# The last batch's second product and the global rows by Strassen's scheme, with result buffers of their own and stores from two queues

## The chip, the cores and the metric

The kernel runs on one core of one Trainium2 chip. A core has five engines, each with an instruction stream of its own: PE (matrix multiplication, with weight loads that overlap it), DVE (element-wise work), ACT (activations and copies), POOL (general work) and SP, which here only issues DMAs. Engines wait for each other through semaphores. Matrix products land in PSUM, eight banks of 512 fp32 columns; everything else lies in SBUF.

The metric is the time of one execution in microseconds (us).

## The reference

Attention with a narrow band and some global rows, then a feed-forward block:

```python
batch, n_heads, seq_l, seq_g, head_dim = (8, 8, 512, 32, 64)
k_all = concatenate([k_g, k_l]);  v_all = concatenate([v_g, v_l])
out_g = softmax(scale * q_g @ k_all.T) @ v_all
s_ll  = where(abs(pos_q - pos_k) <= 32, scale * q_l @ k_l.T, -1e9)
out_l = softmax(concatenate([scale * q_l @ k_g.T, s_ll])) @ v_all
x = concatenate([out_g, out_l], rows)      # per batch 32 + 512 rows, 512 columns (all heads)
h = x @ w_in                               # 512 -> 2048
g = h * clip(h + 3, 0, 6) / 6
out = g @ w_out                            # 2048 -> 512
```

The output has 8 x 544 = 4352 rows of 512 columns in fp32.

## The kernel before, in words

**Tiling.** Work goes by batch b = 0 to 7. Local attention runs in blocks of 128 rows (`local`), the 32 global rows of a batch at once (`global_`). Everything on PE is fp16 with fp32 sums. The result of the attention is turned into `xt[b % 3]`, with the 512 features on partitions in four chunks; the global rows of all eight batches gather in `xg`, 256 rows.

**Feed-forward block.** `ffn_local(b)` has two products. The first (`first`, matmul at line 1003) makes one chunk of 128 of the 2048 hidden features for all 512 rows: four matmuls of 512 columns into one PSUM bank. ACT then makes `t1` out of it (line 1009), and DVE multiplies (line 1013, called a gate here): the result is chunk c of `gl`, fp16, hidden features on partitions. There are two sets, `gl0` (16 tiles, even batches) and `gl1` (one tile of 16 chunks, odd batches). The second product (`second`, line 1029) takes 128 rows and adds up 16 matmuls with `w_out`, 512 columns each, in one bank; ACT or DVE copies the bank into one of three buffers `ot` (line 1040 or 1042), and SP stores it (line 1075). The very last 128 rows are done in two halves of 256 columns. `ffn_global` does the same with the 256 global rows after batch 7: 16 chunks of 256 columns at line 1003, two second products, and four stores of 32 rows each (line 1090).

**Banks.** Three PSUM banks `m` serve these products and, once the last transpose is done, the bank `t` too. Two banks `s` (scores) and two `a` (attention output) belong to the attention.

**Order.** No engine decides anything at run time. A planner (`Plan.run`) goes through all operations with costs written in the code, a pick for PE by keys (`key`, `pick`) and for the other engines by ranks, and writes each engine's instructions down in the order in which it started them. The instruction streams are then fixed; only semaphores decide when an instruction starts. An engine thus waits at an instruction even if the next could go. At the end of the kernel batch 7's first product is followed by the global rows' first product, mixed with second products of batches 6 and 7, and then by second products alone.

**POOL** issues loads and, for the batches from 2 on, copies parts of `vn` to `vs` for the attention (line 645). Its last of these is batch 7's.

Of the kernel before, what the change touches and what calls it, by code (L numbers as in the profile page):

```python
# [10 lines left out]
FP32 = mybir.dt.float32  # L11
# [228 lines left out]
def kernel(  # L240
# [40 lines left out]
    def sbs(name, n, shape, dtype=FP16):  # L281
        return [sb(f"{name}_{i}", shape, dtype) for i in range(n)]
# [49 lines left out]

    plan = Plan()
    add = plan.add
    plan.free = {"m": NM, "t": 2, "s": 4, "a": 4, "t1": NT1, "ot": NOT}
    slots = {"m": list(range(NM)), "t1": list(range(NT1)), "ot": list(range(NOT))}

    def dma(rows, run):

# [29 lines left out]
    def dve(n, fast=1):  # L369
        return 65.0 + n / 0.96 / fast  # L370
# [620 lines left out]


    m1_done = [[] for _ in range(B)]
    m2_done = [[] for _ in range(B)]

    def first(x, n, g, c, deps, rank, kind, free):
        st = {}
# [22 lines left out]
    def second(g, t0, gates, rank, store, kind, cols=slice(0, dm)):  # L1020
# [29 lines left out]
            what="store")  # L1050
        return last

    def ffn_local(b):
        x = xt[b % 3]
        r = b % 2
        parts = ((0, 2), (2, 4)) if b == 0 else ((0, 4),)
        gates = {}
        for part, (j0, j1) in enumerate(parts):
            t0, n = j0 * P, (j1 - j0) * P
            for c in range(NDFF):  # L1060
                free = m2_done[b - 2] if b >= 2 else vperm[0] + vperm[1] if b == 1 else []
                deps = x_op[b][j0:j1] + wi[c // (NDFF // 4)]
                pe, ga = first(lambda m, t0=t0, n=n: x[:, m, t0:t0 + n], n, g_l[r][c][:, t0:t0 + n], c, deps,
                               (b, part, c), "M1", free)
                m1_done[b].append(pe)
                gates[part, c] = ga
        for j in range(NJ):
            row = b * S + Sg + j * P
            part = next(k for k, (j0, j1) in enumerate(parts) if j0 <= j < j1)


            half = dm // 2
            for i, cols in enumerate((slice(0, half), slice(half, dm)) if (b, j) == (B - 1, NJ - 1) else (slice(0, dm),)):
                def store(o, row=row, cols=cols):
                    nc.sync.dma_start(out=out[row:row + P, cols], in_=o[:, 0:cols.stop - cols.start])
                m2_done[b].append(second(g_l[r], j * P, [gates[part, c] for c in range(NDFF)], (b, j + i), store, "M2", cols))

    def ffn_global():
        gates = []
        for c in range(NDFF):  # L1080
            deps = [x_op[b][NJ] for b in range(B)]
            pe, ga = first(lambda m: xg[:, :, m * Sg:(m + 1) * Sg], B * Sg, g_g[c], c, deps, (B, 0, c), "M1",
                           m2_done[B - 2])
            gates.append(ga)
        per = P // Sg
        rows = out.rearrange("(b s) d -> b s d", s=S)
        for i in range(B // per):
            def store(o, i=i):
                for a in range(per):
                    nc.sync.dma_start(out=rows[i * per + a, 0:Sg, :], in_=o[a * Sg:(a + 1) * Sg, :])  # L1090
            second(g_g, i * P, gates, (B, i), store, "M2")
# [27 lines left out]
    EARLY = 60000  # L1119
    KEYS = (30, 30, -20, 40, 27)  # L1120
    REST = 0
    KEYED, GLAST = 0, 0
    state = {"since": 0, "fed": False}
    PIECES = 2 * NDFF

    def key(op):
        if op.key is None:
            r, w = op.rank, op.what
            if w == "Places":
                op.key = -1e9  # L1130
            elif r[0] == B:

                op.key = B * PIECES + (r[2] if w == "M1" else NDFF + 4 * r[1] + r[2])
            elif w == "M1":
                op.key = r[0] * PIECES + 2.0 * (r[2] + r[1] * 0.5)
            elif w[0] == "M":
                op.key = (r[0] + 1) * PIECES + 2.0 * (4 * r[1] + r[2]) + 1
            elif w[0] in "VTG":
                op.key = (r[0] - 1) * PIECES - LEAD - STEP * (2 - 0.25 * min(r[2] * 2, 4)) + KEYS[0]
            else:  # L1140
                op.key = (r[0] - 1) * PIECES - LEAD + STEP * (r[2] + 2 * (r[1] - 1)) + KEYS[1 + (w[0] == "A") + 2 * (w[-1] == "g")]
        return op.key

    def warm():
# [19 lines left out]
    def pick(plan, can):  # L1164
# [76 lines left out]
```

## Time and profile before

| | us |
|---|---|
| median of 3 runs | 330.4 (330.1 to 330.95) |
| the profiled execution | 331.21 |
| its span, first to last instruction | 329.4 |
| PE busy | 318.2 (97%) |
| DVE busy | 239.3 (73%) |
| ACT busy | 237.2 (72%) |
| POOL busy | 174.9 (53%) |

How to read the rows below. A group row has line, engine, operation, output and inputs with shapes, count, then busy time and mean ns of one, then the idle time in front of it and what ended that. A timeline row has start, duration (of all of the row's instructions, merged), engine, line, operation and count; in brackets the idle time of the engine before it and the releaser. PEq, SPq and ACTq rows are the engine's sequencer, for SP the issue of a DMA. The duration of a matmul contains its way through the array, so that successive ones overlap; the pace is told by the starts. A row of the chain has start, duration, engine, output and line. "128x512" is partitions by elements.

### The profile page before, as it was taken

How to read it: one execution, taken by the hardware profiler on the slowest of the kernel's cores; microseconds unless marked ns; L12 is line 12 of the kernel's file. 1: busy time of each engine (PE TensorE's matmuls, PEld its weight loads, DVE VectorE, ACT ScalarE, POOL GpSimd, SP SyncE). 2: the span in 40 equal slices, each digit the busy share in tenths (PEclk: the TensorE clock that was granted, in tenths of full speed). 3: DMA queues.
4: the chain of work that ended last, by engine and by line, in shares of the span. 5: the costliest groups of instructions: out<-in, count | busy, mean ns of one | idle time of the engine just before them, and what ended most of it. 6: DMA issues, size and time to landing. Idle time of an engine off the chain costs nothing.

```text
span 329.4 us, 12254 instructions
## 1 busy us (share of the span) xinstructions
PE 318.2 (97%) x4880; PEld 164.4 (50%) x4880; DVE 239.3 (73%) x987; ACT 237.2 (72%) x571; POOL 174.9 (53%) x278
## 2 busy tenths in 40 slices
PE   8999968999899999999999999999999999999995
PEld 3456756654445544455444544444444444446644
DVE  5699998879985889878898997588414993376400
ACT  3799999848967688689768999979815982365511
POOL 8499353799548879979997998059200000000000
PEclk9999999999999999999999999999999999999999
DMA  8999999998999799959999999598934457200013
GB/s 128 226 204 173 178 235 217 123 180 182 113 136 158 143 116 168 170 120 180 179 111 128 211 102 140 123 136 105 177 99 121 60 109 120 82 34 0 34 57 103
DMA packets 111369, 44.30 MB, mean 134 GB/s; under 512 B 88304, under 2 KB 107088, under 8 KB 111312
## 3 DMA queue, kind: packets, MB, share of 16 engines
q0 software_dynamic: 53136, 17.47, 52.6%
q1 hardware_dynamic: 58176, 26.05, 43.2%
q8 instruction: 38, 0.62, 0.8%
q14 instruction: 19, 0.16, 0.2%
HBM read 35.13 MB, written 8.91 MB: 134 GB/s over the span
## 4 chain that ended last, share of the span: by engine, by line
PE 75%; ACT 9%; DMA 7%; DVE 5%; issue 2%; POOL 1%; ACTq 0%
PE m L1029 30%; PE m L1003 23%; PE t L1029 4%; ACT ex L835 4%; PE t L1003 3%; PE m L1149 3%; DMA win<-in_moe_w_in_dram 3%; PE a L862 3%; DMA et<-ex 3%; PE s L819 2%; ACT t L1009 2%; DVE gl L1013 2%; DMA vn<-in_v_l_dram 1%; ACT vs L643 1%; PE t L883 1%
## 5 line engine op out<-in xcount | busy, mean ns | idle before, releaser
L1003 PE MATMUL m<-xt,win 128*128 128x512 f16 (+1 forms) x536 | 114.3, 354 | 4.2 <-DVE gl L1013 3.1
L1029 PE MATMUL m<-wout,gl 128*128 128x512 f16 (+1 forms) x496 | 117.7, 376 | 0.1
L645 POOL COPY vs<-vn 64x528 f16<-64x528 f16 (+1 forms) x165 | 102.5, 621 | 22.0 <-ACT vn L381 5.7
L1013 DVE SCALAR_TENSOR_TENSOR gl<-t,m 128x512 f16<-128x512 f32 (+1 forms) x147 | 86.3, 601 | 24.2 <-ACT t L1009 23.8
L835 ACT ACTIVATE ex<-sm,mx 128x128 f16<-128x128 f32 x256 | 85.1, 396 | 14.6 <-DVE mx L831 14.1
L1009 ACT ACTIVATE t<-m 128x512 f32<-128x512 f32 (+1 forms) x147 | 76.7, 532 | 19.7 <-PE m L1003 18.7
L1003 PEld LDWEIGHTS <-win 128*128 128x128 f16 x640 | 59.7, 98 | 57.9 <-issue 4.7
L1029 PEld LDWEIGHTS <-gl 128*128 128x128 f16 x560 | 51.7, 98 | 53.5 <-issue 0.4
L831 DVE CUSTOM_DVE_ANT_0 sm<-s,mask 128x128 f32<-128x128 f32 x256 | 60.0, 285 | 7.2 <-PE s L819 5.9
L643 ACT COPY vs<-vn 32x528 f16<-32x528 f16 (+1 forms) x39 | 24.5, 628 | 0.8
L876 DVE TENSOR_TENSOR x<-a,rec 128x256 f16<-128x256 f32 x64 | 24.0, 416 | 0.0
L1040 ACT COPY ot<-m 128x512 f32<-128x512 f32 (+1 forms) x21 | 12.1, 576 | 15.7 <-PE m L1029 15.7
L353 POOL DMA_DIRECT2D vn<-in_v_l_dram x24 | 21.1, 888 | 1.3 <-DMA kn<-in_k_l_dram 0.8
L831 DVE DVE_READ_ACCUMULATOR2_ANT mx<- 128x1 f32 x256 | 21.2, 83 | 0.0
L353 POOL DMA_DIRECT2D vn<-in_v_g_dram x7 | 4.1, 581 | 25.4 <-PE a L965 24.5
L862 PE MATMUL a<-vs,et 128*32 128x65 f16 x1024 | 14.4, 195 | 1.3 <-DMA et<-ex 1.2
L1149 PE MATMUL m<-ident 128*128 128x512 f16 x57 | 15.6, 392 | 0.0
L862 PEld LDWEIGHTS <-et 128*32 128x32 f16 x1024 | 10.2, 96 | 10.9 <-issue 7.3
L1013 DVE SCALAR_TENSOR_TENSOR gl<-t,t 128x512 f16<-128x512 f32 (+1 forms) x13 | 8.1, 624 | 9.7 <-ACT t L1009 9.7
L1029 PE MATMUL t<-wout,gl 128*128 128x512 f16 (+1 forms) x64 | 14.8, 353 | 0.0
L874 DVE RECIPROCAL rec<-a 128x4 f32<-128x4 f32 x64 | 8.5, 167 | 7.9 <-PE a L862 7.9
L353 POOL DMA_DIRECT2D kn<-in_k_l_dram x22 | 14.1, 644 | 0.1
(108 smaller groups left out, 292.4 us busy)
## 6 DMA issues: line engine op xcount, KB each, us to landing
out_dram<-ot SPq DMA_DIRECT2D x31, 256.0 KB, 2.6
vs<-vn SPq DMA_DIRECT2D x14, 264.0 KB, 7.0
qn<-in_q_l_dram POOLq DMA_DIRECT2D x14, 256.0 KB, 8.1
kn<-in_k_l_dram POOLq DMA_DIRECT2D x14, 256.0 KB, 7.1
vn<-in_v_l_dram POOLq DMA_DIRECT2D x24, 128.0 KB, 5.8
win<-in_moe_w_in_dram POOLq DMA_DIRECT2D x4, 512.0 KB, 9.6
wout<-in_moe_w_out_dram POOLq DMA_DIRECT2D x8, 256.0 KB, 11.2
gl<-in_v_l_dram POOLq DMA_DIRECT2D x8, 128.0 KB, 9.3
```

The costliest lines, as they stand in the source:

```text
L353: op = add("POOL", dma(rows, run), lambda: nc.gpsimd.dma_start(out=dst, in_=src), deps, rank, LOAD_LAT + (MARGIN if what[0] in "vqkg" and ...
L643: nc.scalar.copy(out=dst, in_=src)
L645: (nc.vector if o.on == "DVE" else nc.gpsimd).tensor_copy(out=dst, in_=src)
L831: nc.vector.tensor_tensor_reduce(out=sm[i3][h], in0=pss[e][:, p * P:(p + 1) * P], in1=m, scale=-scale, scalar=3.0e38, op0=ALU.add, op1=ALU ...
L835: nc.scalar.activation(out=ex[ie][:, h, :], in_=sm[i3][h], func=EXP, scale=-1.0, bias=mx[i3][h])
L862: nc.tensor.matmul(out=psa[h // 4][q, c0:c0 + D + 1], lhsT=et[k][:, h * P + u * Sg:h * P + (u + 1) * Sg], rhs=vs[r][:, j * UJ + u, h, 0:D ...
L876: nc.vector.tensor_tensor(out=xs[ix][:, 4 * c * D:4 * (c + 1) * D].rearrange("q (h d) -> q h d", d=D), in0=acc[c][:, :, 0:D], in1=rr[c].to ...
L1003: nc.tensor.matmul(out=ps[:, 0:n], lhsT=w_in[:, m, c * P:(c + 1) * P], rhs=x(m), start=(m == 0), stop=(m == NP - 1))
L1009: nc.scalar.activation(out=t1[st["t"]][:, 0:n], in_=pm[st["m"]][:, 0:n], func=RELU, bias=0.5, scale=1.0 / 6.0)
L1013: nc.vector.scalar_tensor_tensor(out=g, in0=t1[st["t"]][:, 0:n], scalar=1.0, in1=pm[st["m"]][:, 0:n], op0=ALU.min, op1=ALU.mult)
L1029: nc.tensor.matmul(out=pm[st["m"]][:, 0:n], lhsT=g[c][:, t0:t0 + P], rhs=w_out[:, c, cols], start=(c == 0), stop=(c == NDFF - 1))
L1149: nc.tensor.matmul(out=pm[slots["m"][0]], lhsT=w, rhs=x)
```

## The change

Batch 7's second product (512 rows) and that of the global rows (256 rows) are done by Strassen's scheme in Winograd's form. Rows, hidden features and output columns are each cut into halves. With A the gates (A11 the upper rows and the lower features) and W the weights `w_out`, the seven products are

```
S1 = A21 + A22   S2 = S1 - A11   S3 = A11 - A21   S4 = A12 - S2      (sums of gates, into vs)
T1 = W12 - W11   T2 = W22 - T1   T3 = W22 - W12   T4 = W21 - T2      (weight differences, into qn and kn)
P1 = A11 W11  P2 = A12 W21  P3 = S4 W22  P4 = A22 T4  P5 = S1 T1  P6 = S2 T2  P7 = S3 T3
U2 = P1 + P6  U3 = U2 + P7  U4 = U2 + P5
C11 = P1 + P2   C12 = U4 + P3   C21 = U3 + P4   C22 = U3 + P5
```

- One product is eight matmuls of 256 columns for 128 rows of each half (`product`). A group of seven makes 256 rows of output (`pair`): two groups for batch 7, one for the global rows. The three groups give 168 matmuls of 256 columns.
- The weight differences are four POOL operations of 2048 elements, planned after the turns of batches 5 to 7 (`weight_sums`).
- The sums of gates are made for two feature chunks of each half at a time, by DVE or POOL as the planner decides (`sevenths`, `both`): 16 operations of 512 elements for batch 7, 16 of 256 for the global rows. To this end the first product makes chunks c and 8 + c one after the other.
- P1 is copied to SBUF by ACT or DVE; U2, U3 and U4 and the four results are additions on DVE with one input in PSUM.
- Results go to five fp32 buffers of 256 columns laid over `vn[0]` (`oq`) and from there to memory. For batch 7 SP issues one store for each; for the global rows ACT and SP issue two stores of 32 rows each.
- The banks of the attention, `s` and `a`, join the `m` banks once the attention is done.
- `gl0` becomes one tile. Batch 6's `ffn_local` is added to the plan ahead of batch 7's `global_`, and global rows have new keys.

In the planned order, POOL does the four weight differences right behind its last copy. Each group of four chunks of batch 7 is followed by its sums: for the first three groups DVE makes S1 and POOL S3, S2 and S4; for the last, DVE makes S1, S2 and S4 and POOL S3. On DVE the last three sums stand ahead of the first global gate. On PE all 16 chunks of batch 7's first product come in a row, then a last quarter of a second product of batch 6, P1, seven global chunks, P6, five chunks, P7, four chunks, and then products alone; the last one is P4 of batch 7's second group. On SP the last stores are C12 of that group, two of the global C21, and C21 of that group.

The diff, cut to its core:

```diff
--- before.py
+++ after.py
@@ tiles
-    g_l = [sbs("gl0", NDFF, [P, Sl]), [gl1[:, c, :] for c in range(NDFF)]]
+    gl0 = sb("gl0", [P, NDFF, Sl])
+    g_all = [gl0, gl1]
+    g_l = [[g[:, c, :] for c in range(NDFF)] for g in g_all]
...
-    plan.free = {"m": NM, "t": 2, "s": 4, "a": 4, "t1": NT1, "ot": NOT}
+    plan.free = {"m": NM, "t": 2, "s": 4, "a": 4, "t1": NT1, "ot": NOT, "oq": 5}
...
+    SEVEN, SUMS = {7: 4, 8: 4}, ("DVE", "POOL")
...
+    HALF, NH = dm // 2, NDFF // 2
+    wt = [qn[k].rearrange("p n c -> p (n c)") for k in range(2)] + [knall[:, k * NH * HALF:(k + 1) * NH * HALF] for k in range(2)]
+    wt = [t.rearrange("p (c f) -> p c f", c=NH) for t in wt]
+    ut = [t.bitcast(FP32) for t in (xt[(B - 3) % 3].rearrange("p n c -> p (n c)"), qT[0].rearrange("d j p q -> d (j p q)"))]
+    oq = vn[0].rearrange("p n h d -> p (n h d)")[:, 0:10 * HALF].bitcast(FP32).rearrange("p (k c) -> p k c", k=5)
+
+    def both(dst, a, b, op, n, engines, deps, rank, what):
+        o = add(engines, tuple(dve(n, 2) if e == "DVE" else 100.0 + 1.9 * n for e in engines), None, deps, rank, lat=220.0, what=what)
+        def emit():
+            (nc.vector if o.on == "DVE" else nc.gpsimd).tensor_tensor(out=dst, in0=a, in1=b, op=op)
...
+    def weight_sums():
+        lo, hi, left, right = slice(0, NH), slice(NH, NDFF), slice(0, HALF), slice(HALF, dm)
...
+        for k, (a, d, x) in enumerate(((w_out[:, lo, right], w_out[:, lo, left], ()), (w_out[:, hi, right], wt[0], (0,)),
+                                       (w_out[:, hi, right], w_out[:, lo, right], ()), (w_out[:, hi, left], wt[1], (1,)))):
+            wt_op[k] = both(wt[k], a, d, ALU.subtract, n, ("POOL",), free + [wt_op[i] for i in x], (B, 5, k), f"wt{k}")
+
+    def sevenths(b, g, n, gates, into, free, store, banks):
+        st_ = into.rearrange("p u h d -> p (u h d)")[:, 0:4 * NH * n].rearrange("p (s c t) -> p s c t", s=4, c=NH)
+        up, dn = slice(0, n), slice(n, 2 * n)
+        for c in range(0, NH, 2):
+            lo, hi = slice(c, c + 2), slice(NH + c, NH + c + 2)
+            deps = [gates[i] for i in (c, c + 1, NH + c, NH + c + 1)] + free
+            for k, (x, y, op, by) in enumerate(((g[:, lo, dn], g[:, hi, dn], ALU.add, ()), (st_[:, 0, lo], g[:, lo, up], ALU.subtract, (0,)),
+                                                (g[:, lo, up], g[:, lo, dn], ALU.subtract, ()), (g[:, hi, up], st_[:, 1, lo], ALU.subtract, (1,)))):
+                o = both(st_[:, k, lo], x, y, op, 2 * n, SUMS, deps + [done[i] for i in by], (b, 0, 6, c, k), f"sum{b}.{k}")
...
+        for i in range(n // P):
+            pair(b, i, n, g, st_, sums, gates, store, banks)
+
+    def pair(b, i, n, g, s_, sums, gates, store, banks):
...
+        def product(m, x, lhs, rhs, deps, take=None):
+            def emit():
+                if take is not None:
+                    st[take] = slots["m"].pop(0)
+                for c in range(NH):
+                    nc.tensor.matmul(out=at(x), lhsT=lhs(c), rhs=rhs(c), start=c == 0, stop=c == NH - 1)
...
+        def plus(dst, a, x, deps, bank=None):
+                nc.vector.tensor_tensor(out=dst, in0=a(), in1=at(x), op=ALU.add)
...
+        def outs(row, cols, x, a, deps, bank):
+                so["o"] = slots["oq"].pop(0)
+                nc.vector.tensor_tensor(out=oq[:, so["o"], :], in0=a, in1=at(x), op=ALU.add)
...
+            half = [add("ACT", 900.0, lambda: store(i, row, cols, oq[:, so["o"], :], nc.scalar), [op], (-1,), lat=0.0, what="store")] if b == B else []
...
+        p1 = product(0, "X", gt(0, a1), wo_(0, left), g1 + wo, 0)
...
+        p6 = product(1, "Y", su(1), wt_(1), sums[1] + [wt_op[1]], 1)
+        u2 = plus(ub[1], lambda: ub[0], "Y", [p6, cx], None if two else 1)
+        p7 = product(2, "W", su(2), wt_(2), sums[2] + [wt_op[2]] + ([cx] if two else []), None if two else 2)
+        u3 = plus(ub[2], lambda: ub[1], "W", [p7, u2])
+        p5 = product(3, "V", su(0), wt_(0), sums[0] + [wt_op[0]] + ([u2] if two else []), None if two else 3)
+        u4 = plus(ub[3], lambda: ub[1], "V", [p5, u2])
+        c22 = outs(1, right, "V", ub[2], [p5, u3], None)
+        p2 = product(4, "X", gt(NH, a1), wo_(NH, left), g2 + [cx] + ([u3] if two else []))
+        c11 = outs(0, left, "X", ub[0], [p2], None if two else 0)
+        p3 = product(5, "V", su(3), wo_(NH, right), sums[3] + [c22, u4])
+        c12 = outs(0, right, "V", ub[3], [p3, u4], 1 if two else 3)
+        p4 = product(6, "W", gt(NH, a2), wt_(3), [u3, wt_op[3]] + ([c11] if two else []))
+        c21 = outs(1, left, "W", ub[2], [p4], 0 if two else 2)
@@ ffn_local
+                place = 2 * (c % NH) + c // NH if b in SEVEN else c
...
+        if b in SEVEN:
+            def quarter(i, row, cols, o, queue):
+                r0 = b * S + Sg + (2 * row + i) * P
+                queue.dma_start(out=out[r0:r0 + P, cols], in_=o)
+            sevenths(b, g_all[r], Sl // 2, [gates[0, c] for c in range(NDFF)], vs[r], [], quarter, SEVEN[b])
+            return
@@ ffn_global
+            def quarter(i, row, cols, o, queue):
+                for a in range(per // 2) if queue is nc.scalar else range(per // 2, per):
+                    queue.dma_start(out=rows[row * per + a, 0:Sg, cols], in_=o[a * Sg:(a + 1) * Sg, :])
+            sevenths(B, g_all[B % 2], B * Sg // 2, gates, vs[B % 2], m2_done[B - 2], quarter, SEVEN[B])
+            return
@@ order of the work
+        if b == B - 1 and SEVEN:
+            weight_sums()
+            ffn_local(b - 1)
         global_(b)
-        ffn_local(b)
+        if b != B - 2 or not SEVEN:
+            ffn_local(b)
...
+    GLOBALS = (0, 0.5, 12)
...
-                op.key = B * PIECES + (r[2] if w == "M1" else NDFF + 4 * r[1] + r[2])
+                op.key = B * PIECES + (GLOBALS[0] + GLOBALS[1] * r[2] if w == "M1" else GLOBALS[2] + 4 * r[1] + r[2])
...
+    for k, (r, banks) in enumerate((("s", pss), ("a", psa))):
+        pm.extend(banks)
+        add("POOL", 0.0, lambda k=k: slots["m"].extend((NM + 1 + 2 * k, NM + 2 + 2 * k)), [u for u in plan.ops if r in u.give], (-9,),
+            0.0, take=(r,) * 4, give=("m", "m"), what="bank")
```

More of the change, by code (lines that the diff above doesn't have):

```diff
@@ L993 @@
     m1_done = [[] for _ in range(B)]
-    m2_done = [[] for _ in range(B)]
+    m2_done = [[] for _ in range(B + 1)]
+    SEVEN, SUMS = {7: 4, 8: 4}, ("DVE", "POOL")
     def first(x, n, g, c, deps, rank, kind, free):
@@ L1062, in ffn_local @@
                 deps = x_op[b][j0:j1] + wi[c // (NDFF // 4)]
+                place = 2 * (c % NH) + c // NH if b in SEVEN else c
                 pe, ga = first(lambda m, t0=t0, n=n: x[:, m, t0:t0 + n], n, g_l[r][c][:, t0:t0 + n], c, deps,
-                               (b, part, c), "M1", free)
+                               (b, part, place), "M1", free)
                 m1_done[b].append(pe)
                 gates[part, c] = ga
+        if b in SEVEN:
[4 more added lines that the diff above has]
+            return
         for j in range(NJ):
@@ L1081, in ffn_global @@
             deps = [x_op[b][NJ] for b in range(B)]
-            pe, ga = first(lambda m: xg[:, :, m * Sg:(m + 1) * Sg], B * Sg, g_g[c], c, deps, (B, 0, c), "M1",
-                           m2_done[B - 2])
+            pe, ga = first(lambda m: xg[:, :, m * Sg:(m + 1) * Sg], B * Sg, g_g[c], c, deps,
+                           (B, 0, 2 * (c % NH) + c // NH if B in SEVEN else c), "M1", m2_done[B - 2])
             gates.append(ga)
```

73 lines of the change are left out of this document (70 added, 3 removed).

## The prediction

> **What bounds the kernel now.** I read the page's busy line first, then the same engines cut into the stages of the end (windows), then the chain that ended last.
>
> ```profile
> PE 318.2 (97%) x4880; PEld 164.4 (50%) x4880; DVE 239.3 (73%) x987; ACT 237.2 (72%) x571; POOL 174.9 (53%) x278
> PEclk9999999999999999999999999999999999999999
> ...
> 283.50:298.00 14.50, 14.50 (x69) 6.61 (x68) 9.62 (x14) 10.05 (x17) 0.00 (x0) 1.00 0.11 40
> 298.00:312.00 14.00, 14.00 (x98) 9.38 (x97) 7.52 (x17) 6.99 (x19) 0.00 (x0) 1.00 0.05 19
> 312.00:326.10 14.10, 14.05 (x82) 7.75 (x80) 0.42 (x1) 2.79 (x6) 0.00 (x0) 1.00 0.25 74
> ...
> 282.65 0.97 PE t L1029 x4
> 283.62 1.73 PE m L1003 x8
> 293.12 2.59 PE m L1003 x12
> 312.19 9.50 PE m L1029 x44
> 325.17 0.89 PE m L1029 x8
> 326.06 0.03 ACTq L1040
> 326.13 0.37 ACT ot L1040
> ```
>
> The window rows give, after the stretch and its length, PE, weight loads, DVE, ACT and POOL in turn. From 283.5 us to 326.1 us PE has no gap, the clock is full, POOL does nothing, and DVE is busy 9.62, 7.52 and 0.42 us in three stretches of about 14 us. The chain is PE from end to end; only a copy and a store stand behind it. So here a microsecond of matmul taken away is a microsecond of the span, as long as DVE, which gets work, doesn't take PE's place.
>
> The instruction orders of the two kernels are the same on all five engines up to the first matmul of batch 7's first product (283.46 us below), but for POOL, which gets its new work behind its last copy. Everything that the change can do lies behind that point.
>
> **Terms, step by step.**
>
> *Matmuls.* These rows give the pace: a start to the next start, since the ends overlap.
>
> ```profile
> 283.46 1.89 PE L1003 MATMUL m<-xt,win 128*128 128x512 f16 x8
> 324.14 0.60 PE L1029 MATMUL m<-wout,gl 128*128 128x256 f16 x4
> 324.57 0.60 PE L1029 MATMUL t<-wout,gl 128*128 128x256 f16 x4
> 325.01 1.04 PE L1029 MATMUL m<-wout,gl 128*128 128x256 f16 x8
> 325.65 1.22 SPq L1075 DMA_DIRECT2D out_dram<-ot  x2
> 326.13 0.37 ACT L1040 COPY ot<-m 128x256 f32<-128x256 f32 x1 [0.50 <-PE m L1029]
> ```
>
> A 512-column matmul costs 2.59 / 12 = 0.216 us (chain), a 256-column one (325.01 - 324.14) / 8 = 0.109 us, with its own weights each time, so a column costs the same in both. Removed: second product of batch 7, 48 of 512 and 32 of 256 columns, and of the global rows, 32 of 512: 80 x 0.216 + 32 x 0.109 = 20.75 us. Added: 7 products x 3 pairs x 8 = 168 of 256 columns: 168 x 0.109 = 18.27 us. PE gets 2.48 us shorter; its last matmul, which ended its 8 x 0.109 at 325.88, ends at 323.40. The bounds of this term are narrow, since the rows have the very shape.
>
> *The order.* Batch 7's first product now runs its 16 chunks in one go (chunks c and 8+c side by side), with banks of the scores and of the attention output in use as well. Then a last piece of batch 6, one product, 7 global chunks, one product, and so on. No matmul is added by that.
>
> *Weight differences on POOL* (four of 2048 elements). POOL ends its last copies at 231.91 + 1.30 = 233.2 us:
>
> ```profile
> L645 POOL COPY vs<-vn x165: 612/620/675, 15.8 to 232.6; 64x528 f16<-64x528 f16 x90, 32x528 f16<-32x528 f16 x75
> 231.91 1.30 POOL L645 COPY vs<-vn 32x528 f16<-32x528 f16 x2
> ```
>
> A POOL operation with two inputs is nowhere in this trace. Bounds from the copy of 528 elements, 0.62 us: not less than the copy (0.60 us for 512 elements), and, since both inputs have to be read, hardly over twice that (1.20 us). I take the upper one, because the rows show no POOL work that is cheaper by the element. Then the four take 4 x 4 x 1.2 = 19 us and end near 253 us; the first use is at 302 us. Cost nothing; 49 us of cover. The Trainium skill (GPSIMD Engine Reference, Elementwise side-by-side cycle accounting) measures 4497 ns for an fp32 add of 2048 elements; by that page I estimate 1.12 us for 512, and the sum would be the same.
>
> *Sums of gates.* 16 operations of 512 elements for batch 7 and 16 of 256 for the global rows; the order gives DVE 6 and 7, POOL 10 and 9. On DVE the nearest row is a 16-bit copy of 512 elements.
>
> ```profile
> L383 DVE COPY xt<-t 128x512 f16<-128x512 f16 x12 | 5.0, 416 | 0.1
> L1013 DVE SCALAR_TENSOR_TENSOR gl<-t,m 128x256 f16<-128x256 f32 x45 | 17.5, 416 | 6.6 <-ACT t L1009 6.3
> 268.25 0.68 DVE L1013 SCALAR_TENSOR_TENSOR gl<-t,t 128x512 f16<-128x512 f32 x1
> 268.89 0.69 DVE L1013 SCALAR_TENSOR_TENSOR gl<-t,m 128x512 f16<-128x512 f32 x1
> 289.50 2.75 PE L1003 MATMUL m<-xt,win 128*128 128x512 f16 x12
> 290.57 0.60 ACT L1009 ACTIVATE t<-m 128x512 f32<-128x512 f32 x1 [0.27 <-PE m L1003]
> 291.20 0.69 DVE L1013 SCALAR_TENSOR_TENSOR gl<-t,m 128x512 f16<-128x512 f32 x1 [0.17 <-ACT t L1009]
> ```
>
> So 0.42 us for 512, some 0.29 for 256 (bounds: the copy's rate, and 0.69 and 0.42 of the gates). A gate is 0.64 us from start to start (268.25 to 268.89) and ends 1.53 us behind its four matmuls (289.50 + 0.86 to 291.20 + 0.69). Four chunks take PE 3.45 us; DVE needs 4 x 0.64 + 0.42 = 2.98. The first group of four is ready at 283.46 + 3.45 + 1.53 = 288.44. PE comes to its second Strassen product at 283.46 + 13.81 + 0.86 + 0.87 + 3.05 = 302.05 (16 chunks, the piece, a product, 7 global chunks); this needs the bank of the first global chunk, whose gate stands on DVE behind all six sums. DVE's work from 288.44 to the end of that gate: 12 x 0.64 + 6 x 0.42 + 0.42 = 10.6 us, so 299.1 by work alone: 3.0 us of slack.
>
> That slack is what the shared use with POOL eats. This is what the trace shows of it, in the first batches, where both copy from SBUF to SBUF:
>
> ```profile
> 24.64 0.61 POOL L645 COPY vs<-vn 64x528 f16<-64x528 f16 x1
> 25.85 1.98 POOL L645 COPY vs<-vn 64x528 f16<-64x528 f16 x3
> 26.00 1.30 DVE L645 COPY vs<-vn 32x528 f16<-32x528 f16 x2
> 28.89 0.29 DVE L645 COPY vs<-vn 32x528 f16<-32x528 f16 x1
> ```
>
> A DVE copy is 0.29 us beside little POOL work, and 0.65 behind POOL's copies: it waits until POOL's instruction is over. Whether an add with two SBUF inputs does so too, no row shows; bounds: no wait, or the rest of POOL's sum, up to 1.2 us. I reckon with the wait. If DVE goes first in each group, POOL needs 0.42 + 3 x 1.2 = 4.02 us a group against PE's 3.45, falls behind, and DVE's next sum waits for it. POOL's third group ends at 288.44 + 3 x 4.02 = 300.5; then come three DVE sums and the gate, 3 x 0.38 + 0.42: 302.1, just when PE wants the bank. Cost 0 to 0.3 us with the half-size sums behind; I take 0.1. The Trainium skill (SBUF State Buffer, Who interferes with whom) states this wait for just this pair, a DVE instruction with two SBUF inputs against a GpSimd one that reads SBUF; it speaks against the change. By it the sum is the one above; without it the 0.1 us would be 0.
>
> *Additions of the products.* 9 adds and 12 results on DVE, 256 columns, fp32 with one PSUM input: 0.42 us each as the 256-column gate, 8.8 us, and 3 copies of 0.37 on ACT. They lie in the last 20 us, where DVE had 0.42 us of work in 14 us and PE gives one product in 0.87 us. Cost nothing but for the last one.
>
> *The end.* In the old kernel the last copy starts 0.25 us behind PE (325.88 to 326.13), and the last store is issued at 326.5:
>
> ```profile
> L1075 SPq DMA_DIRECT2D out_dram<-ot x33: 332/351/649, 67.5 to 326.5; - x33
> DMA to landing us min/median/max: 1.7/2.4/4.9
> L1090 SPq DMA_DIRECT2D out_dram<-ot x8: 322/412/433, 318.9 to 325.0; - x8
> ```
>
> Now the last add ends at 323.40 + 0.25 + 0.42 = 324.07, but SP has work ahead of this store: one quarter of batch 7 (its add ends 0.87 us earlier, at 323.20; 0.35 us), then two stores of the global block (0.41 each): free at 324.4. So 326.5 becomes 324.4. ACT issues eight global stores, which no row prices; SP's 0.41 is the nearest, and four issues' worth of error there is covered by the two products still to come. Results go to five buffers. The last add, at 323.65, reuses the one of the result five products earlier, which DVE gives, as its second operation there, at 323.40 - 5 x 0.87 + 0.25 + 0.42 + 0.38 = 320.1: with 2.4 us to landing that holds, with 4.9 it would cost 1.4.
>
> *Sum.* 2.48 - 0.35 (SP's queue) - 0.05 (add for copy) - 0.1 = 2.0 us. The profiled execution took 331.21 us for a span of 329.4, 0.8 over the median of 330.4; I take the difference off the median: 328.4 us.
>
> **Rivals.** A difference below 0.3%, 1.0 us, can't be told from none.
>
> Slower: POOL takes the shared read first. At each of the four group ends both engines become ready with the same gate. If POOL starts first, DVE waits 1.2 us four times: 10.6 + 4.8 = 15.4 us from 288.44, and the bank is free at 303.9, 1.8 us late. In the global rows five of DVE's seven sums meet POOL again, 0.3 to 0.6 us each, and the gates behind them hold PE's banks: 1.5 us more. 328.4 + 3.2 = 331.6 us. The first part alone decides when 4 x d exceeds 3.0 + 2.0, d = 1.25 us a sum. For it: the 26.00 row, where DVE is the one who waits. Against it: DVE has just run the gate and needs no message from another engine.
>
> Part of the gain: DVE first, but POOL's sum at 1.3 to 1.4 us. Its three groups then end 9 x 0.1 to 9 x 0.2 us later: 0.9 to 1.8 us; 329.5 us. For it: two inputs may cost more than two copies; against: a copy's fixed part would count once.
>
> No change: the end eats it. If a store lands after 4.9 us instead of 2.4, the buffer of the last add is late by the 1.4 us: 329.8 us. For it: the slowest landing in the row; against: it is from busy stretches, and the window rows show the DMAs near idle.
>
> **How the numbers follow.** The forecast 0.60 (its own range 327.9 to 329.0), part of the gain 0.18, no change 0.05, POOL first 0.17. Faster by over 0.3%: the forecast and a third of the second, 0.66; within: the rest of the second and the no change, 0.17; slower: 0.17, where a POOL sum over 1.2 us would go on to 334. Range 327.7 to 331.0: it leaves out about 0.04 below and 0.15 above, the worse part of POOL first.
>
> **What will show it.** PE's last matmul near 323.4 and no PE wait on DVE behind 283 us: right. A PE wait at 302 to 304 us on a global gate, with DVE's sums at 1 us instead of 0.42, names the shared read; POOL sums over 1.2 us name POOL's rate; a DVE idle on a store ahead of the last add names the buffers. The 256-column products should keep 0.109 us. A PE pace slower than that, or gaps between products on their additions, would prove the matmul term wrong.

## The result, and the profile after

| | before | after |
|---|---|---|
| median, us | 330.4 | 328.74 |
| the profiled execution, us | 331.21 | 328.15 |
| its span, us | 329.4 | 326.4 |

The ratio of the times, after to before, is 0.9936 with a 95% interval of 0.9908 to 0.9964: 2.1 us faster, between 1.2 and 3.0. The medians are over eleven runs of each kernel, one of them slow on either side; the ratio is that of the means of the ten others, 330.6 and 328.5 us. The forecast was 328.4 us.

The page's busy line of the changed kernel, then the same three stretches as in the prediction (the columns are PE, weight loads, DVE, ACT, POOL, clock, DMA share, GB/s; the last stretch ends earlier, at 324 us):

```profile
PE 316.0 (97%) x4936; PEld 169.9 (52%) x4936; DVE 253.5 (78%) x1021; ACT 234.7 (72%) x567; POOL 208.8 (64%) x301
...
283.50:298.00 14.50, 14.50 (x73) 6.95 (x72) 12.82 (x19) 10.14 (x17) 9.94 (x9) 1.00 0.06 20
298.00:312.00 14.00, 14.00 (x131) 12.54 (x129) 12.92 (x33) 7.14 (x19) 7.77 (x11) 1.00 0.10 34
312.00:324.00 12.00, 10.61 (x98) 9.26 (x95) 6.14 (x15) 0.00 (x0) 0.00 (x0) 1.00 0.33 102
```

PE still has no gap until it is done, at full clock. DVE, which had 9.62, 7.52 and 0.42 us of work in these stretches, now has 12.82, 12.92 and 6.14, and POOL, which had none, 9.94 and 7.77.

The changed file has its lines a little lower: 1007 is the first product (1003 before), 1033 the second (1029), 1125 a Strassen product, 1072 a sum of gates or of weights, 1149 a result, 1219 and 1246 the stores of batch 7 and of the global rows. The end of the chain that ended last (start, duration, engine, output, line) is PE's products and one addition:

```profile
320.97 0.76 PE m L1125 x7
321.74 0.89 PE s L1125 x8
322.62 0.02 issue
322.65 0.42 DVE vn L1149
```

The two spans differ by 3.0 us, but not all of that is the change. The instruction orders are the same up to the first matmul of batch 7's first product (but for POOL's new work), and this matmul starts at 283.46 us in the trace of before and at 282.44 in that of after. Over the traces in the table below, all with that same order in front, it starts anywhere from 281.38 to 284.09 us. So the number to read is the stretch behind that start. PE in the changed kernel:

```profile
282.44 1.89 PE L1007 MATMUL s<-xt,win 128*128 128x512 f16 x8
301.05 1.04 PE L1125 MATMUL m<-qn,vs 128*128 128x256 f16 x8
321.57 1.04 PE L1125 MATMUL s<-kn,gl 128*128 128x256 f16 x8
```

The last eight matmuls take 8 x 0.109 = 0.87 us by the pace of the prediction's rows. From the first matmul of the stretch to PE's end: before 325.01 + 0.87 - 283.46 = 42.42 us, after 321.57 + 0.87 - 282.44 = 40.00, 2.42 less. To the end of the span: before 329.4 - 283.46 = 45.94, after 326.4 - 282.44 = 43.96, 1.98 less. The stretch of the changed kernel came out at 40.00 and 40.14 us in two traces, where the time of a kernel can't tell 1 us.

### The profile page after: what moved, and what is told of

It is laid out like the page before. It is cut to its first block, busy times and chain, and to the rows that moved or that the text cites. A ratio compares the mean times of both kernels' runs of the same rounds, so it can differ in the third digit from the quotient of the medians.

```text
span 326.4 us, 12465 instructions
## 1 busy us (share of the span) xinstructions
PE 316.0 (97%) x4936; PEld 169.9 (52%) x4936; DVE 253.5 (78%) x1021; ACT 234.7 (72%) x567; POOL 208.8 (64%) x301
## 4 chain that ended last, share of the span: by engine, by line
PE 78%; DVE 8%; ACT 5%; DMA 3%; issue 2%; POOL 1%; ACTq 0%; POOLq 0%
PE m L1033 26%; PE m L1007 24%; PE a L864 3%; PE m L1125 3%; PE s L821 3%; PE t L1007 3%; PE t L1033 2%; PE s L1007 2%; DVE gl L1017 2%; DVE sm L833 2%; ACT t L1013 2%; PE a L1007 2%; DMA qn<-in_q_l_dram 2%; ACT vs L645 2%; PE s L1125 2%
## 5 line engine op out<-in xcount | busy, mean ns | idle before, releaser
L1007 PE MATMUL m<-xt,win 128*128 128x512 f16 (+1 forms) x504 | 106.9, 353 | 3.5 <-DVE gl L1017 3.0
L1033 PE MATMUL m<-wout,gl 128*128 128x512 f16 x416 | 100.7, 380 | 0.1
L1017 DVE SCALAR_TENSOR_TENSOR gl<-t,m 128x512 f16<-128x512 f32 (+1 forms) x129 | 76.7, 609 | 14.5 <-ACT t L1013 14.2
L1013 ACT ACTIVATE t<-m 128x512 f32<-128x512 f32 (+1 forms) x129 | 68.1, 540 | 12.2 <-PE m L1007 11.4
L1033 PEld LDWEIGHTS <-gl 128*128 128x128 f16 x448 | 40.7, 98 | 45.4 <-issue 0.3
L1072 POOL TENSOR_TENSOR vs<-gl 128x256 f16<-128x256 f16 (+1 forms) x9 | 8.3, 924 | 38.5 <-DVE gl L1017 38.5
L821 PEld LDWEIGHTS <-qT 64*32 64x32 f16 x1024 | 8.1, 91 | 11.6 <-issue 11.1
L821 PE MATMUL s<-kT,qT 64*32 64x128 f16 x1024 | 13.8, 219 | 0.3 <-ACT eg L940 0.3
```

Of the source, the lines that this page charges most:

```text
L821: nc.tensor.matmul(out=pss[e][u * Sg:(u + 1) * Sg, p * P:(p + 1) * P], lhsT=qT[r][rows, j, p, u * Sg:(u + 1) * Sg], rhs=kT[r][rows, p, k0: ...
L1007: nc.tensor.matmul(out=ps[:, 0:n], lhsT=w_in[:, m, c * P:(c + 1) * P], rhs=x(m), start=(m == 0), stop=(m == NP - 1))
L1013: nc.scalar.activation(out=t1[st["t"]][:, 0:n], in_=pm[st["m"]][:, 0:n], func=RELU, bias=0.5, scale=1.0 / 6.0)
L1017: nc.vector.scalar_tensor_tensor(out=g, in0=t1[st["t"]][:, 0:n], scalar=1.0, in1=pm[st["m"]][:, 0:n], op0=ALU.min, op1=ALU.mult)
L1033: nc.tensor.matmul(out=pm[st["m"]][:, 0:n], lhsT=g[c][:, t0:t0 + P], rhs=w_out[:, c, cols], start=(c == 0), stop=(c == NDFF - 1))
```

## The experiments

The table has the stretch of every kernel: the start of batch 7's first matmul, the start of PE's last row, and what lies between the former and PE's end (last start + 0.87 - first start; the last row of the kernel without Strassen products has 32 matmuls, so + 3.49).

| kernel | first | last | stretch, us | ratio to before, 95% |
|---|---|---|---|---|
| before | 283.46 | 325.01 | 42.42 | 1 |
| after | 282.44 | 321.57 | 40.00 | 0.9936 (0.9908 to 0.9964) |
| rest_only | 282.06 | 320.99 | 42.42 | 0.9995 (0.9974 to 1.0015) |
| batch7_only | 282.70 | 322.89 | 41.06 | 0.9962 (0.9933 to 0.9991) |
| global_only | 284.07 | 324.83 | 41.63 | 1.0006 (0.9982 to 1.0029) |
| pool_longer | 281.90 | 321.14 | 40.11 | one execution, 327.74 us |
| pool_one_long | 283.63 | 327.00 | 44.24 | one execution, 333.61 us |
| pool_memset | 281.38 | 320.51 | 40.00 | one execution, 327.13 us |
| after_again | 282.45 | 321.72 | 40.14 | 0.9943 (0.9912 to 0.9974) |
| act_stores_look | 282.77 | 321.90 | 40.00 | one execution, 328.34 us |
| sums_dve | 284.09 | 323.22 | 40.00 | 0.9922 (0.9892 to 0.9952) |
| sums_dve_again | 283.18 | 322.31 | 40.00 | 0.9920 (0.9896 to 0.9945) |
| last_by_act | 281.90 | 321.04 | 40.01 | 0.9904 (0.9870 to 0.9938) |

`after_again` is the changed kernel once more, beside other experiments on their chip:

> The changed kernel once more, on the chip of the run with all global stores by ACT: ratio to before 0.994 within 0.003; the stretch from batch 7's first matmul to PE's end 40.0 us, no PE wait behind 283 us. Rival (the gain in the first timing came from the part ahead of batch 7's first matmul, whose length differs from run to run): the ratio is nearer 0.998.

### Is it the matmuls? One part of the change at a time

```diff
-    SEVEN, SUMS = {7: 4, 8: 4}, ("DVE", "POOL")
+    SEVEN, SUMS = {}, ("DVE", "POOL")             # rest_only
+    SEVEN, SUMS = {7: 4}, ("DVE", "POOL")         # batch7_only
+    SEVEN, SUMS = {8: 4}, ("DVE", "POOL")         # global_only
```

> All of the change but the scheme itself: no batch and no global rows by seven products, so no sums and no weight differences; the attention's banks join the others, gl0 is one tile, the global rows have the new keys. Theory (only the matmul time counts, PE has no gap): PE's time from batch 7's first matmul to the end of its last stays at the 42.42 us of before, within 0.1 us, and the time at 330.4 us, within 0.3%. Rival (the new order and the additional banks bring the gain): that stretch gets 1 us or more shorter, and the time is near 329 us.

> The scheme for batch 7 alone. Theory: the matmuls lose 48 x 0.216 + 32 x 0.109 = 13.86 us and gain 112 x 0.109 = 12.2 us; the stretch from batch 7's first matmul to PE's end is 42.42 - 1.65 = 40.8 us, time 328.9 us. Rival (a fixed part comes from the order or the end, not from the matmuls): the stretch is 40.0 us, as with both.

> The scheme for the global rows alone. Theory: 32 x 0.216 = 6.91 us of matmuls become 56 x 0.109 = 6.10 us; the stretch is 42.42 - 0.81 = 41.6 us, time 329.7 us. Rival (sums of the global rows, right ahead of their use, are what PE waits for): a PE wait on DVE or POOL behind 300 us, stretch 42.4 us or more.

PE's rows of rest_only, of batch7_only and of global_only:

```profile
282.06 1.89 PE L1007 MATMUL s<-xt,win 128*128 128x512 f16 x8
320.99 3.66 PE L1033 MATMUL m<-wout,gl 128*128 128x256 f16 x32
```

```profile
301.45 1.03 PE L1125 MATMUL m<-qn,vs 128*128 128x256 f16 x8
...
321.01 1.04 PE L1125 MATMUL a<-wout,gl 128*128 128x256 f16 x8
322.02 1.03 PE L1125 MATMUL m<-wout,vs 128*128 128x256 f16 x8
322.89 1.04 PE L1125 MATMUL t<-kn,gl 128*128 128x256 f16 x8
```

```profile
284.07 1.89 PE L1007 MATMUL s<-xt,win 128*128 128x512 f16 x8
324.83 1.04 PE L1033 MATMUL a<-wout,gl 128*128 128x256 f16 x8
```

Everything but the products (the new banks, the one tile for `gl0`, the new order of batch 6 and the global rows) gives 0.00 us in the stretch and a ratio of 0.9995. Strassen for batch 7 alone should take 48 x 0.216 + 32 x 0.109 - 112 x 0.109 = 1.65 us; the stretch is 1.36 us shorter, and two small gaps of PE, ahead of the rows at 301.45 and 322.02, make up the rest (from 321.01 to 322.02 are 1.01 us for matmuls of 0.87; the last section has the cause of both). For the global rows alone it should be 32 x 0.216 - 56 x 0.109 = 0.81; it is 0.79. The two parts give 2.15 us together, the whole 2.42. In time batch 7's part shows (0.9962). The part of the global rows does not: global_only took 330.16 us instead of the expected 329.7, and its interval, 0.9982 to 1.0029, just leaves out the 0.9975 that 0.81 us would give. So this part of the gain rests on the stretch of one execution, and on the whole change, whose stretch is shorter than that of batch7_only; the times don't confirm it.

### How does POOL hold DVE? A longer chain, one long read, writes alone

The prediction had DVE go first in each group and its last sums hang on the end of POOL's chain of sums. The trace of after says otherwise. DVE's and POOL's instructions in the four groups of batch 7 (two timelines of the same kernel):

```profile
287.56 0.62 DVE L1072 TENSOR_TENSOR vs<-gl 128x512 f16<-128x512 f16 x1
...
290.96 1.08 DVE L1072 TENSOR_TENSOR vs<-gl 128x512 f16<-128x512 f16 x1
294.53 1.36 DVE L1072 TENSOR_TENSOR vs<-gl 128x512 f16<-128x512 f16 x1
298.32 0.42 DVE L1072 TENSOR_TENSOR vs<-gl 128x512 f16<-128x512 f16 x1
298.84 1.21 DVE L1072 TENSOR_TENSOR vs<-vs,gl 128x512 f16<-128x512 f16 x1
300.15 0.42 DVE L1072 TENSOR_TENSOR vs<-gl,vs 128x512 f16<-128x512 f16 x1
300.49 0.42 DVE L1017 SCALAR_TENSOR_TENSOR gl<-t,m 128x256 f16<-128x256 f32 x1
```

```profile
286.75 1.16 POOL L1072 TENSOR_TENSOR vs<-gl 128x512 f16<-128x512 f16 x1 [34.62 <-DVE gl L1017]
...
290.61 1.15 POOL L1072 TENSOR_TENSOR vs<-gl 128x512 f16<-128x512 f16 x1
...
294.46 1.15 POOL L1072 TENSOR_TENSOR vs<-gl 128x512 f16<-128x512 f16 x1
...
298.32 1.44 POOL L1072 TENSOR_TENSOR vs<-gl 128x512 f16<-128x512 f16 x1
```

A DVE sum takes 0.42 us with POOL quiet, and up to 1.36 us where it starts right behind the start of a POOL sum (294.46, 294.53); at 298.32 both start together, DVE takes its 0.42 and POOL 1.44 instead of 1.15. So one waits for the other, and the wait stands inside the duration, not as idle time. In the first three groups POOL is first: S3 needs only the lower chunks, of which the second is the third gate of a group, while S1 needs all four. In the fourth group the two are ready together, and who goes first differs from execution to execution: in after_again POOL starts at 298.32, DVE at 298.33, and this time it is DVE's sum that takes 1.44 us. Three kernels ask what the wait hangs on.

pool_longer adds ten POOL copies of 256 elements, one behind each of POOL's sums for batch 7, 4.7 us more of chain in small pieces:

```diff
+            if o.on == "POOL" and what[:4] == "sum7":
+                nc.gpsimd.tensor_copy(out=pad, in_=a[:, 0, 0:256])
```

> The changed kernel with a copy of 256 elements behind each of POOL's ten sums of batch 7, some 0.35 us each; every stream is else the same. In the changed kernel the first global gate ends at 300.91 us and PE wants its bank at 301.05, 0.14 us of slack. Theory (DVE's sums wait for POOL through the shared read): POOL's three groups take 3 x 3 x 0.35 = 3.15 us longer, DVE's sums behind them wait as long, PE's second Strassen product waits some 3 us for a global gate, and the stretch goes from 40.0 to 43 us or more. Rival (DVE waits for POOL only where it needs POOL's result): the second product needs POOL's eighth sum, at 297.13 + 8 x 0.35 = 299.9 us, the third its tenth, at 299.76 + 3.5 = 303.3 us against 304.1; no PE wait, stretch 40.0 us.

pool_one_long adds a single POOL addition of 2048 elements ahead of the second group's sums:

```diff
+            if o.on == "POOL" and what == "sum7.2" and rank[3] == 2:
+                nc.gpsimd.tensor_tensor(out=pad.rearrange("p (n c) -> p n c", n=4), in0=gl1[:, 0:4, :], in1=w_out[:, 0:4, :], op=ALU.add)
```

> The changed kernel with one more POOL operation: an add of 2048 elements with two SBUF inputs (4.07 us, as the weight differences took), ahead of POOL's sums of the second group of batch 7; its result is used by nothing. In all it is less POOL time than the ten copies of the run before (4.1 us against some 4.6), but in one instruction. Theory (a DVE sum waits for the POOL instruction in progress, and for nothing else of POOL's backlog): DVE's sum of that group starts some 0.3 us behind it and takes 0.42 + 3.7 = 4.1 us instead of 1.08; the gates behind it are late, and PE waits 1 to 3 us, first on a gate; the stretch from batch 7's first matmul to PE's end goes from 40.0 to 41 to 43 us. Rival (POOL's time counts only through its results): the eighth sum ends near 301.2 us, in time for the product that reads it, no PE wait, stretch 40.0 to 40.2 us as with the ten copies.

pool_memset leaves POOL's sums of gates out (so these products aren't the reference's) and has POOL fill their place with constants instead, 18 times 512 elements, which only writes:

```diff
+            if o.on == "POOL" and what[:3] == "sum":
+                for _ in range(6 if what == "sum7.1" else 0):
+                    nc.gpsimd.memset(a, 0.125)
+                return
```

> The changed kernel without POOL's sums of gates (left out, so the products read other values); in their place POOL fills the S1 sums of each of the first three groups six times over, which writes SBUF and reads nothing. DVE's instructions are the same. Theory (it is POOL's reading that DVE's second input meets): every DVE sum of 512 elements takes 0.42 us, also those that run while POOL writes (1.08 and 1.36 us in the changed kernel). Rival (any POOL work holds DVE up): sums beside the fills take up to the length of one fill longer. PE has no wait in either case, stretch 40.0 us.

The timelines of pool_longer, of pool_one_long and of pool_memset:

```profile
293.86 1.15 POOL L1073 TENSOR_TENSOR vs<-gl,vs 128x512 f16<-128x512 f16 x1
294.96 0.59 POOL L1075 COPY pad<-gl 128x256 f16<-128x256 f16 x1
293.88 1.41 DVE L1073 TENSOR_TENSOR vs<-gl 128x512 f16<-128x512 f16 x1
```

```profile
291.81 4.06 POOL L1074 TENSOR_TENSOR kT<-gl,wout 128x2048 f16<-128x2048 f16 x1
292.15 4.00 DVE L1075 TENSOR_TENSOR vs<-gl 128x512 f16<-128x512 f16 x1
...
298.52 0.82 PE L1128 MATMUL m<-wout,gl 128*128 128x256 f16 x6
300.44 0.28 PE L1128 MATMUL m<-wout,gl 128*128 128x256 f16 x1 [1.10 <-DVE gl L1017]
301.63 0.28 PE L1128 MATMUL m<-wout,gl 128*128 128x256 f16 x1 [0.91 <-DVE gl L1017]
```

```profile
287.04 10.33 POOL L1074 MEMSET vs<- 128x512 f16 x18 [36.41 <-DVE vs L1076]
...
289.90 0.43 DVE L1076 TENSOR_TENSOR vs<-gl 128x512 f16<-128x512 f16 x1
293.36 0.42 DVE L1076 TENSOR_TENSOR vs<-gl 128x512 f16<-128x512 f16 x1
```

In pool_longer DVE's sum ends at 293.88 + 1.41 = 295.29, right behind the end of the POOL sum that was running (295.01), while POOL's next instruction, already begun at 294.96, waits in its turn (0.59 us where its fellows take 0.39). So DVE waits for one instruction and gets in ahead of the next; 4.7 us more in POOL's queue left the stretch at 40.11 us, no longer than in after_again (40.14). This ended the theory that DVE waits for POOL's whole chain, which expected some 3 us. In pool_one_long the same DVE sum waits out the rest of the one long addition, 4.00 us, the gates behind it come late, and PE waits for them at the first Strassen product: 4.24 us lost, more than expected (the last section has the reason). In pool_memset all DVE sums of 512 elements take 0.42 or 0.43 us, the two shown among them, which lie inside 10.33 us of POOL's writing. So it is POOL's reading that holds DVE, for the instruction in progress. The Trainium skill (SBUF — State Buffer, Who interferes with whom) says just this: a DVE instruction with two SBUF inputs contends with a GpSimd one that reads SBUF, not with one that only writes, and whoever issues first has the lock for its whole instruction. The traces agree with each part (4.00 us beside the read of 4.06 us, 0.42 beside the writes).

### Is POOL's share of the sums needed?

```diff
-    SEVEN, SUMS = {7: 4, 8: 4}, ("DVE", "POOL")
+    SEVEN, SUMS = {7: 4, 8: 4}, ("DVE",)
```

> All sums of gates on DVE, none on POOL; the planner writes a new order for it, which spreads the sums between the gates. No POOL instruction reads SBUF while they run. Theory (DVE has room once nothing holds it up): up to the first global gate DVE has 12 gates x 0.64 + some 13 sums x 0.38 + 0.42 = 13.0 us behind the first group, against 13.6 us that PE takes, and 0 to 0.7 us are lost in the global rows, where 15 gates, 15 sums and 4 additions come to 10.4 us; the stretch is 40.0 to 40.8 us, time near 328.5 us. Rival (POOL's share is needed): DVE's gates come late, PE waits for them, stretch 42 us or more, time 330.5 us or more.

> The kernel of sums_dve once more, on the chip of last_by_act: gate sums on DVE alone. Expected by the theory that only PE's matmul time counts: no PE wait behind 283 us, 40.0 us from batch 7's first matmul to PE's end, 43.9 to 44.0 us to the end of the span, ratio 0.992 to 0.995. Rival (DVE, without idle time in 300 to 312 us, gives a bank late in some executions): a PE wait at the second Strassen product and 40.3 us or more.

The rows of sums_dve by line and by stretch:

```profile
L1072 DVE TENSOR_TENSOR vs<-gl 128x512 f16<-128x512 f16 x8 | 3.3, 421 | 0.1
L1072 DVE TENSOR_TENSOR vs<-gl 128x256 f16<-128x256 f16 x8 | 2.2, 287 | 0.0
...
304.00:308.00 4.00, 4.00 (x39) 3.59 (x37) 4.00 (x16) 2.60 (x7) 0.00 (x0) 1.00 0.01 2
```

All sums now take 0.42 or 0.29 us, DVE has no idle time there, PE none either, and the stretch is 40.00 us twice. The ratios, 0.9922 and 0.9920, can't be told from those of after and after_again (0.9936, 0.9943). POOL's help bought nothing: without it DVE has 10 x 0.42 + 9 x 0.29 = 6.8 us more of sums, but no waits inside them and no exchange with POOL.

### The end: who issues the last stores

act_stores (and act_stores_look, the same kernel, from which the trace is) has ACT issue all stores of the global rows, so that SP's last store finds its queue free:

```diff
-                store(i, row, cols, oq[:, so["o"], :], nc.sync)
+                store(i, row, cols, oq[:, so["o"], :], nc.scalar if b == B else nc.sync)
...
-                for a in range(per // 2) if queue is nc.scalar else range(per // 2, per):
+                for a in range(per):
```

> All four stores of each global quarter by ACT, none by SP; SP has only batch 7's. In the changed kernel the last add ended at 323.07 us and its store was issued by SP at 323.65, behind two global stores. Theory (SP's queue delays the end): the last store is issued at once, 0.55 us earlier, so that from batch 7's first matmul to the last issue it takes 40.65 us instead of 41.2; time 328.2 us against the changed kernel's 328.7, by the interval hardly to be told apart. Rival (ACT's queue takes its place): ACT issues four stores of 0.42 us for the global rows' last quarter from 321.3 to 323.0 us, they land behind SP's last one, and the span does not get shorter.

> The kernel with all global stores by ACT once more, for a profile that can be read beside the others. Theory (SP's queue delays the end): SP issues its last store right behind the last add, so that from batch 7's first matmul to that issue it takes 40.65 us instead of 41.2, and the span behind the issue stays at 2.7 us. Rival (ACT's four stores of the global rows' last quarter take its place): the issue is early, but the span goes on for more than 3.0 us behind it.

last_by_act, on the base of sums_dve, gives ACT only the four stores of the last global result:

```diff
-                for a in range(per // 2) if queue is nc.scalar else range(per // 2, per):
+                n_act = per if (row, cols.start) == (1, 0) else per // 2
+                for a in range(n_act) if queue is nc.scalar else range(n_act, per):
```

> Gate sums on DVE alone (as in sums_dve), and all four stores of the last global block of results issued by ACT; the other global blocks stay shared between SP and ACT. Theory (the end is set by the queue that issues last, and ACT, which issued its last store in the changed kernel's profile near 321.8 us, has room for two more): SP's last issue comes some 0.55 us earlier, ACT ends its issues about 0.5 us behind the last add, and from batch 7's first matmul to the end of the span it is 43.4 to 43.5 us against 43.96 us; the ratio to the kernel before is then near 0.992, not to be told apart in time from sums_dve on the same chip. Rival (as in act_stores_look, the ACT queue takes SP's place): four issues of 0.42 us behind the last add are 1.7 us, more than SP's 0.58 us, and the stretch gets 0.5 to 1.1 us longer, 44.4 to 45 us.

The issues of stores in after, in act_stores_look and in last_by_act (the row's duration covers all its issues and the time between them):

```profile
322.62 0.94 SPq L1246 DMA_DIRECT2D out_dram<-vn  x2
323.65 0.37 SPq L1219 DMA_DIRECT2D out_dram<-vn  x1
316.56 5.67 ACTq L1246 DMA_DIRECT2D out_dram<-vn  x8
```

```profile
316.89 7.54 ACTq L1247 DMA_DIRECT2D out_dram<-vn  x16
```

```profile
321.68 1.23 SPq L1219 DMA_DIRECT2D out_dram<-vn  x2
315.91 6.75 ACTq L1247 DMA_DIRECT2D out_dram<-vn  x10
322.11 0.42 DVE L1149 TENSOR_TENSOR vn<-qT,s 128x256 f32<-128x256 f32 x1 [0.45 <-PE s L1125]
```

In after the last addition ends at 322.65 + 0.42 = 323.07, and SP is still issuing two stores of the global rows until 322.62 + 0.94 = 323.56: its last store comes at 323.65, 0.58 us late. With all global stores on ACT, SP is on time, but ACT issues until 316.89 + 7.54 = 324.43, and the span ends 326.6 - 282.77 = 43.83 us behind the first matmul: only 0.13 us less than in after. That is the rival's answer: ACT's queue has taken the place of SP's. act_stores has a ratio of 0.9943 (0.9919 to 0.9968), the same as after_again beside it. With only the last four on ACT, both queues end together: ACT at 315.91 + 6.75 = 322.66, SP at 321.68 + 1.23 = 322.91, the addition at 322.53. From the first matmul to the end of the span it is 325.3 - 281.90 = 43.40 us, as expected: 0.56 less than after, and 0.52 less than its base, sums_dve_again (327.1 - 283.18 = 43.92). Its median is 327.4 us and its ratio the lowest of all; the times alone can't tell it from sums_dve_again beside it (0.9904 against 0.9920), the stretch of one execution does.

## Why the prediction was right, step by step

- **Matmuls.** Forecast 2.48 us less, measured 2.42 in the stretch. rest_only shows that this is the only term with a gain; the 256-column products kept their 0.87 us for eight.
- **The order.** Forecast nothing, rest_only 0.00 us.
- **Weight differences.** They ended at 252.1 us, forecast 253; the first use is at 301.05. Hidden. One takes 4.06 us and a sum of 512 elements 1.155, against the 1.20 that I took from two copies. This is the row of the last one, from POOL's timeline of after:

```profile
248.06 4.07 POOL L1072 TENSOR_TENSOR kn<-wout,qn 128x2048 f16<-128x2048 f16 x1
```

- **Sums of gates.** The sizes were right (0.42 and 0.29 us on DVE without POOL in the way), and so was the wait for the rest of POOL's instruction. The step that failed is "If DVE goes first in each group" and what hung on it, that DVE's last sums wait for "POOL's third group". POOL goes first, as one rival had it, yet DVE waits only for what is left of one instruction: six sums took 0.62 + 1.08 + 1.36 + 0.42 + 1.21 + 0.42 = 5.11 us instead of 2.52, that is 2.6 us of the 3.0 us of slack. The first global gate ends at 300.49 + 0.42 = 300.91, P6 starts at 301.05: no cost in this execution, with 0.14 us to spare. In after_again, where DVE lost the fourth meeting too, PE waited 0.14 us at this place (rows in the last section). So the forecast 0.1 had the right size, but by luck. That the bank came free "just when PE wants the bank" was the right moment from a wrong mechanism, as pool_longer shows: the chain got 4.7 us longer and the moment stayed. The rows from which the wait was read were also weaker than the prediction has it: while the DVE copy at 28.89 us took its 0.29, a POOL copy ran from 28.40 to 29.02. The wait of an addition with two SBUF inputs is shown by the experiments, not by those rows.
- **Rival: POOL first, 331.6 us.** Its order came true in the first three groups, its price didn't: it charged a whole POOL sum of 1.2 us per meeting, where DVE's sums in these groups took 0.20, 0.66 and 0.94 us longer.
- **Rival: POOL's sum at 1.3 to 1.4 us.** It is 1.155.
- **Additions.** 0.42 us each, and in the changed kernel PE never waits for one.
- **The end.** The term was too small: SP's last store is issued 0.58 us behind the last addition, forecast 0.33 (324.4 against 324.07). To that issue the stretch got 1.83 us shorter, forecast 2.1; behind it the span goes on 326.4 - 323.65 = 2.75 us instead of 329.4 - 326.5 = 2.9, which gave back 0.15.
- **Rival: a late landing.** The stores of the new buffers land in 1.6 to 1.7 us at the median, and no PE wait followed.
- **The sum.** 1.98 us from the stretch, forecast 2.0; the ratio says 2.1. So close a match is partly luck: the matmuls gave 0.06 us less and SP's queue took some 0.2 more than forecast, the sums of gates took 0.1 less and the last landing 0.15 less.

## What to carry to other kernels

Where the chain of waits is one engine from end to end, count its instructions at their measured pace, and then walk each other engine up to the place where it is wanted back: the slack there, here 3.0 us, decides whether help from a further engine costs or not. DVE sums with two SBUF inputs and POOL work that reads SBUF don't add up as two engines: a meeting costs DVE up to the rest of one POOL instruction (here up to 1.02 us beside sums of 1.155 us, and 3.58 us beside the one of 4.06), so long POOL instructions are the dangerous ones, and doing all on DVE can be as good. At the very end look at each queue's issues behind the last result, and split them so that the queues end together.

## What the runs showed of the hardware that was not expected

**In one execution the clock fell after a short idle.** pool_one_long lost 4.24 us although PE's idle was 2.35: from 298.52 + 6 x 0.109 = 299.17 to 300.44, and from 300.44 + 0.11 = 300.55 to 301.63. Here are pool_one_long's stretches (the number ahead of the last two, which are DMA share and GB/s, is the granted clock; in after it is 1.00 there):

```profile
300.00:302.00 2.00, 0.65 (x5) 0.43 (x6) 2.00 (x4) 0.05 (x1) 1.92 (x3) 1.00 0.35 131
302.00:304.00 2.00, 2.00 (x13) 1.48 (x11) 1.88 (x3) 1.09 (x3) 2.00 (x2) 0.57 0.00 0
304.00:306.00 2.00, 2.00 (x13) 1.48 (x11) 1.90 (x5) 1.00 (x3) 0.43 (x1) 0.58 0.00 0
```

These are means: in windows of a quarter of a us the clock is 1.00 up to 302.25 and 0.50 from 302.50 to 305.50. From the last matmul of the first Strassen product (301.63) to the start of P6 (306.48) it takes 4.85 us, in after 301.05 - (297.12 + 7 x 0.109) = 3.17, so 1.68 us more. With the 2.35 of idle, and 0.21 in gaps ahead of 298.52, that is the 4.24. The Trainium skill (TensorE: Matmul & The Clock Gate, Why this matters for your kernels) advises no PE idle of more than about 3 us between bursts; here two gaps of 1.27 and 1.08 us, with one matmul between them, came ahead of the fall. A single gap of 1.52 us, ahead of the matmul at 42.80 us in the trace of before, left the clock at 1.00. So the wait of PE cost nearly twice its length here; this is one execution, and that the idle caused the fall is not tested further.

**The small gaps ahead of P6 come from the same shared read.** In batch7_only, pool_longer and after_again PE has a gap of 0.11 to 0.14 us ahead of P6, for which the profile names no wait. The rows of after_again show what ends it:

```profile
298.32 1.16 POOL L1072 TENSOR_TENSOR vs<-gl 128x512 f16<-128x512 f16 x1
298.33 1.44 DVE L1072 TENSOR_TENSOR vs<-gl 128x512 f16<-128x512 f16 x1
300.62 0.60 PE L1007 MATMUL m<-xg,win 128*128 128x256 f16 x4
300.73 0.42 DVE L1017 SCALAR_TENSOR_TENSOR gl<-t,m 128x256 f16<-128x256 f32 x1
301.20 1.03 PE L1125 MATMUL m<-qn,vs 128*128 128x256 f16 x8
```

PE is done with its four matmuls at 300.62 + 0.44 = 301.06, but the first global gate, whose bank P6 needs, ends at 300.73 + 0.42 = 301.15, and P6 starts 0.05 us behind it. In batch7_only and pool_longer P6 also starts 0.05 us behind the end of this gate. In after the gate ended at 300.91, early enough. The other gap of batch7_only, ahead of 322.02, is not from the shared read: it ends 0.06 us behind the addition that gives C22 (321.55 + 0.41 = 321.96), whose bank the next product uses.

**What stays open.** No run settles which of two engines gets the read when they start within 0.01 us of each other, whether the fall of the clock comes again, or why the gain of the global rows does not show in the times of global_only.
